# Grouped-query attention over a KV cache: loads of K, V and wo with wider DRAM pieces

## The chip, the core and the metric

The kernel runs on one core of a Trainium2 chip. The metric is the device time in microseconds (us) of one execution. The profile shows the engines of the core: PE (TensorE, with its weight loads shown apart as PEld), DVE (VectorE), ACT (ScalarE), POOL (GpSimd) and SP, the engine that here only issues DMAs. Sixteen DMA engines move the data between DRAM and SBUF.

## What is computed

It is one attention block for decoding with a cache, in bf16, with B = 32 batches of Sq = 4 new tokens, D = 1024, 32 query heads, 4 kv heads, 2048 cached positions and head size 128.

```python
B, Sq, D = 32, 4, 1024
Hq, Hkv, Sk, Dh = 32, 4, 2048, 128
q = (x @ wq).reshape(B, Sq, Hq, Dh)            # x: [B, Sq, D], wq: [D, Hq*Dh]
k = repeat(k_cache, Hq // Hkv, axis=heads)     # k_cache, v_cache: [B, Hkv, Sk, Dh]
v = repeat(v_cache, Hq // Hkv, axis=heads)
p = softmax(q @ k.T * Dh ** -0.5, axis=-1)
o = p @ v
out = o.reshape(B, Sq, Hq * Dh) @ wo           # wo: [Hq*Dh, D]
```

The two caches hold 67 MB each, wq and wo 8.4 MB each; everything is read from DRAM once.

## The kernel before

The engines have a program each, written out by hand and tied together by counting semaphores; a function `plan` numbers the events of each engine beforehand, and `wait_ev` waits for such a number. One batch at a time goes through five steps on TensorE:

- `do_kt_fills`: K arrives with positions on the partitions and has to be transposed. For each of the 4 kv heads two fills of 8 transposes each go into one bank of a ring of four PSUM banks (ps_a, ps_b, ps_c, ps_o; line 320), and DVE or ACT copies each bank to KT_sb (lines 452 and 454).
- The scores: 16 matmuls into ps_s (line 405), all 32 heads times 4 tokens as 128 rows.
- DVE takes the row maximum (line 489), and ACT the exponential with its sum (line 547) into pp_sb.
- `do_tr_fills`: 16 matmuls against a diagonal matrix transpose and scale the probabilities (line 336), through the same ring.
- `do_pv`: 64 matmuls of the probabilities with V (line 354), copied to oT_sb.

The order on TensorE in batch i is: scores of i, `do_pv` of i - 1, `do_kt_fills` of i + 2, `do_tr_fills` of i. Ahead of the loop stand the transposition of x, the fills of batches 0 and 1 and the projection of q (line 379); after it come 64 matmuls with wo (line 426) and the store of the output.

**Loads.** K_sb has two buffers of a whole batch (2 MB) and V_sb three. In SBUF partition p of a batch and head holds positions 16p to 16p + 15, which are 4 KB in a row of DRAM. K comes in one DMA for each kv head (512 KB), and each head has a semaphore of its own; V comes in one DMA for each batch (2 MB). wo comes in 32 DMAs of 256 KB, one for each query head, in rows of 2 KB, into the SBUF space of wq. ACT issues the K of batches 0 and 1; SP issues everything else, in this order: x, the four parts of wq, K2, V0, K3, V1, and then for each batch b from 2 on V(b), K(b + 2) and one wo block. Before V(b) SP waits until `do_pv` of b - 3 has freed the buffer (line 273), and before K(b) for the last fill of b - 2 (line 278). Before the first wo block it waits for the end of the projection of q (line 266).

The lines of the access patterns and of the wait for V are these:

```python
def k_src(b):                                                    # L229
    return k_cache[b].rearrange("g (p t) d -> p g (t d)", p=128)
...
eng.dma_start(V_sb[:, vs, :, :], v_src(b)).then_inc(s_v[vs], 16) # L274
...
eng.wait_ge(s_v[vs], 16 * (b // NVB + 1))                        # L347, do_pv
```

## Time and profile before

| | |
|---|---|
| time, median of 2 runs | 413.37 us (413.29 to 413.44) |
| the profiled execution | 413.86 us, of which the span of the instructions is 412.1 us |
| granted clock of TensorE | 0.917 of full speed, mean |
| busy: PE, PEld | 316.0 us (77%), 257.4 us (62%) |
| busy: DVE, ACT, POOL | 247.1 us (60%), 198.6 us (48%), 0.7 us |
| DMA | 152.33 MB in 44437 packets, mean 370 GB/s over the span |

Busy time is the time in which an engine executes instructions; its share of the span is an average over parts of the kernel with different limits. The span runs from the first to the last instruction; the time of an execution also has some 1.8 us around it. The profile cuts the span into 40 slices of 10.3 us and gives for each the busy tenths of every engine and the GB/s that the DMA engines moved. Its chain is the work that ended last, followed back from the last instruction to whatever released each step.

### The profile page before, as it was taken

The page shows a single profiled execution, that of the slowest core. Times are in us where ns is not written, and L with a number is a line of the kernel's source. Part 1 is how long each engine was busy: PE and PEld are TensorE (multiplying, and loading weights), DVE is VectorE, ACT ScalarE, POOL GpSimd, SP SyncE. Part 2 cuts the span into 40 slices and gives each one's busy share as a digit, 9 for nine tenths or more (in the row PEclk, how much of TensorE's full clock was granted, in tenths as well). Part 3 has the DMA queues.
Part 4 walks back from the last instruction along what each step waited for, and adds up shares of the span by engine and source line. Part 5 has one row for each costly group of instructions (what it writes and reads, how often), then busy time and mean ns, then how long its engine had stood idle before and what let it go on. Part 6 is the DMA issues. An engine that isn't in the chain of part 4 may idle for free.

```text
span 412.1 us, 12650 instructions
## 1 busy us (share of the span) xinstructions
PE 316.0 (77%) x5448; PEld 257.4 (62%) x5448; DVE 247.1 (60%) x390; ACT 198.6 (48%) x230; POOL 0.7 (0%) x6
## 2 busy tenths in 40 slices
PE   4489787887886986897787787777788787776596
PEld 3489576676665864775576665656576566665442
DVE  2114686775865786586677577667657667754500
ACT  1213655643645475455555355555535555534400
POOL 0000000000000000000000000000000000000000
PEclk9889998988989899699989899999979989978679
DMA  8999999999999999999999999999999999996000
GB/s 303 400 387 400 409 409 405 407 406 407 406 407 408 405 408 406 407 407 407 406 406 407 407 403 407 406 406 406 406 408 406 407 408 406 405 406 251 6 2 25
DMA packets 44437, 152.33 MB, mean 370 GB/s; under 512 B 3168, under 2 KB 3168, under 8 KB 44384
## 3 DMA queue, kind: packets, MB, share of 16 engines
q1 hardware_dynamic: 43232, 147.34, 90.5%
q10 hardware_dynamic: 1152, 4.19, 2.6%
q8 instruction: 44, 0.72, 0.7%
q14 instruction: 9, 0.07, 0.0%
HBM read 151.26 MB, written 0.26 MB: 368 GB/s over the span
## 4 chain that ended last, share of the span: by engine, by line
DMA 61%; PE 25%; SPq 5%; ACT 4%; issue 3%; DVE 2%; ACTq 0%; DVEq 0%
DMA K_sb<-in_k_cache_dram 55%; DMA w_sb<-in_wq_dram 6%; PE ps_c L320 4%; SPq L280 4%; PE ps_s L426 4%; PE ps_o L320 3%; PE ps_a L320 3%; ACT KT_sb L454 3%; PE ps_b L320 3%; PE ps_s L379 3%; DVE mx L489 2%; PE ps_s L405 1%; PE ps_o L354 1%; PE ps_a L336 1%; PE ps_o L336 1%
## 5 line engine op out<-in xcount | busy, mean ns | idle before, releaser
L547 ACT ACTIVATE pp_sb<-ps_s,negmx 128x2048 bf16<-128x2048 f32 x32 | 63.0, 1967 | 98.5 <-DVE negmx L492 98.5
L489 DVE TENSOR_REDUCE mx<-ps_s 128x1 f32<-128x2048 f32 x32 | 73.3, 2292 | 43.3 <-PE ps_s L405 43.3
L320 PE MATMUL ps_a<-ident,K_sb 128*128 128x128 bf16 x512 | 45.9, 240 | 31.9 <-DMA K_sb<-in_k_cache_dram 27.6
L354 PEld LDWEIGHTS ps_o<-pp_sb,V_sb 128*128 128x128 bf16 x2048 | 53.8, 96 | 17.9 <-issue 17.9
L454 ACT ACTIVATE KT_sb<-ps_a 128x1024 bf16<-128x1024 bf16 x32 | 32.7, 1023 | 59.1 <-PE ps_a L320 59.1
L354 PE MATMUL ps_o<-pp_sb,V_sb 128*128 128x32 bf16 x2048 | 57.2, 177 | 3.9 <-issue 3.0
L320 PEld LDWEIGHTS ps_a<-ident,K_sb 128*128 128x128 bf16 x512 | 34.8, 109 | 38.1 <-DMA K_sb<-in_k_cache_dram 32.5
L320 PE MATMUL ps_c<-ident,K_sb 128*128 128x128 bf16 x512 | 46.3, 242 | 12.6 <-DMA K_sb<-in_k_cache_dram 11.5
L452 DVE COPY KT_sb<-ps_b 128x1024 bf16<-128x1024 bf16 x64 | 43.9, 686 | 9.8 <-PE ps_b L320 9.0
L320 PEld LDWEIGHTS ps_c<-ident,K_sb 128*128 128x128 bf16 x512 | 35.7, 110 | 18.9 <-DMA K_sb<-in_k_cache_dram 17.2
L320 PE MATMUL ps_o<-ident,K_sb 128*128 128x128 bf16 x512 | 45.0, 238 | 2.2 <-DVE KT_sb L452 2.0
L320 PE MATMUL ps_b<-ident,K_sb 128*128 128x128 bf16 x512 | 45.3, 239 | 1.0 <-issue 1.0
L320 PEld LDWEIGHTS ps_o<-ident,K_sb 128*128 128x128 bf16 x512 | 36.4, 109 | 3.7 <-DVE KT_sb L452 3.0
L320 PEld LDWEIGHTS ps_b<-ident,K_sb 128*128 128x128 bf16 x512 | 36.8, 109 | 1.3 <-issue 1.2
L452 DVE COPY KT_sb<-ps_a 128x1024 bf16<-128x1024 bf16 x32 | 22.1, 691 | 24.8 <-PE ps_a L320 24.8
L405 PE MATMUL ps_s<-KT_sb,QT_sb 128*32 128x512 bf16 x512 | 34.3, 388 | 2.5 <-ACT QT_sb L530 0.8
L454 ACT ACTIVATE KT_sb<-ps_c 128x1024 bf16<-128x1024 bf16 x32 | 32.7, 1023 | 7.1 <-PE ps_c L320 7.0
L452 DVE CAST pp_sb<-ps_a 128x512 bf16<-128x512 f32 x32 | 22.1, 692 | 20.2 <-PE ps_a L336 20.2
L454 ACT ACTIVATE KT_sb<-ps_o 128x1024 bf16<-128x1024 bf16 x32 | 32.7, 1021 | 0.0
L452 DVE COPY KT_sb<-ps_c 128x1024 bf16<-128x1024 bf16 x32 | 22.1, 690 | 8.4 <-PE ps_c L320 8.3
L336 PE MATMUL ps_o<-diag,pp_sb 128*128 128x128 bf16 x128 | 13.2, 227 | 14.9 <-ACT KT_sb L454 14.9
L452 DVE CAST pp_sb<-ps_c 128x512 bf16<-128x512 f32 x32 | 22.1, 690 | 3.7 <-PE ps_c L336 1.4
(34 smaller groups left out, 245.2 us busy)
## 6 DMA issues: line engine op xcount, KB each, us to landing
V_sb<-in_v_cache_dram SPq DMA_DIRECT2D x32, 2048.0 KB, 19.2
K_sb<-in_k_cache_dram SPq DMA_DIRECT2D x120, 512.0 KB, 15.8
w_sb<-in_wq_dram SPq DMA_DIRECT2D x4, 2048.0 KB, 23.6
w_sb<-in_wo_dram SPq DMA_DIRECT2D x32, 256.0 KB, 14.7
K_sb<-in_k_cache_dram ACTq DMA_DIRECT2D x8, 512.0 KB, 10.6
pp_sb<-in_x_dram SPq DMA_DIRECT2D x1, 256.0 KB, 4.2
out_dram<-pp_sb SPq DMA_DIRECT2D x1, 256.0 KB, 2.0
```

The source lines that it names most:

```text
L280: eng.dma_start(K_sb[:, ks, g, :], k_src(b)[:, g, :]).then_inc(s_k[ks][g], 16)
L320: ins = eng.transpose(dst[:, q * 128:(q + 1) * 128], K_sb[:, ks, g, t * Dh:(t + 1) * Dh], ident[:, :],)
L336: ins = eng.matmul(dst[:, q * 128:(q + 1) * 128], lhsT=P_sb[:, t * 128:(t + 1) * 128], rhs=diag[:, b % 2, :], start=True, stop=True,)
L354: ins = eng.matmul(ps_o[:, 32 * g:32 * (g + 1)], lhsT=V_sb[:, vs, g, t * Dh:(t + 1) * Dh], rhs=PT_sb[:, t, 32 * g:32 * (g + 1)], start=(t ...
L379: ins = eng.matmul(ps_s[:, col:col + 128], lhsT=wq_sb[:, kt, h * Dh:(h + 1) * Dh], rhs=xT_sb[:, kt, :], start=(kt == 0), stop=(kt == KT - 1),)
L405: ins = eng.matmul(ps_s[32 * g:32 * (g + 1), c * 512:(c + 1) * 512], lhsT=QT_sb[:, i, REP * g:REP * (g + 1), :], rhs=KT_sb[:, kts, g, c * ...
L426: ins = eng.matmul(ps_s[:, c * 512:(c + 1) * 512], lhsT=oT_sb[:, h, :], rhs=wo_view[:, h, c * 512:(c + 1) * 512], start=(h == 0), stop=(h ...
L452: ins = eng.tensor_copy(dst, src)
L454: ins = eng.activation(dst, src, ACT.Copy)
L489: ins = eng.tensor_reduce(mx[:, i:i + 1], ps_s[:, :], AX.X, ALU.max)
L547: ins = eng.activation(P_sb, ps_s[:, :], ACT.Exp, bias=negmx[:, i:i + 1], scale=scale, accum_out=ssum[:, i:i + 1],)
```

## The change

A helper `_load` issues a DMA whose source and destination have different shapes and the same number of elements. The source patterns of K and V get 32 rows of 16 KB in place of 128 rows of 4 KB, and that of a wo block 16 rows of 16 KB in place of 128 rows of 2 KB; the destinations stay at 128 partitions with 4 KB (2 KB) each. Read in order, the elements of both sides match, so each byte goes to the same place as before. V is issued head by head, four DMAs of 512 KB for a batch, all of which raise the same semaphore; `do_pv` waits for four times the count.

```diff
+def _load(nc, eng, dst, src):
+    return eng.add_instruction(mybir.InstDMACopy(
+        name=nc.get_next_instruction_name(),
+        engine=eng.engine,
+        mode="Copy",
+        queue={mybir.EngineType.SP: "qSPDynamicHW", mybir.EngineType.Activation: "qActDynamicHW"}[eng.engine],
+        cce_op=ALU.bypass,
+        ins=[eng.lower_ap_dma(src)[0]],
+        outs=[eng.lower_ap_dma(dst)[0]],
+    ))
...
         def k_src(b):
-            return k_cache[b].rearrange("g (p t) d -> p g (t d)", p=128)
+            return k_cache[b].rearrange("g (p t) d -> p g (t d)", p=32)
         def v_src(b):
-            return v_cache[b].rearrange("g (p t) d -> p g (t d)", p=128)
+            return v_cache[b].rearrange("g (p t) d -> p g (t d)", p=32)
...
-                    eng.dma_start(wo_view[:, h, :], wo[h * 128:(h + 1) * 128, :]).then_inc(s_wo, 16)
+                    _load(nc, eng, wo_view[:, h, :], wo[h * 128:(h + 1) * 128, :].rearrange("(p r) n -> p (r n)", r=8)).then_inc(s_wo, 16)
...
-                eng.dma_start(V_sb[:, vs, :, :], v_src(b)).then_inc(s_v[vs], 16)
+                for g in range(G):
+                    _load(nc, eng, V_sb[:, vs, g, :], v_src(b)[:, g, :]).then_inc(s_v[vs], 16)
...
-                    eng.dma_start(K_sb[:, ks, g, :], k_src(b)[:, g, :]).then_inc(s_k[ks][g], 16)
+                    _load(nc, eng, K_sb[:, ks, g, :], k_src(b)[:, g, :]).then_inc(s_k[ks][g], 16)
...
-                eng.wait_ge(s_v[vs], 16 * (b // NVB + 1))
+                eng.wait_ge(s_v[vs], 16 * G * (b // NVB + 1))
...
-                    eng.dma_start(K_sb[:, b % NKB, g, :], k_src(b)[:, g, :]).then_inc(s_k[b % NKB][g], 16)
+                    _load(nc, eng, K_sb[:, b % NKB, g, :], k_src(b)[:, g, :]).then_inc(s_k[b % NKB][g], 16)
```

The last pair of lines is ACT's issue of K0 and K1.

## The prediction

> **What bounds the kernel now.** I read the page's DMA rows first, then the chain of waits, then the table of busy time by stretch, and last the waits of TensorE on K_sb and the DMA issues.

> ```profile
> DMA  8999999999999999999999999999999999996000
> GB/s 303 400 387 400 409 409 405 407 406 407 406 407 408 405 408 406 407 407 407 406 406 407 407 403 407 406 406 406 406 408 406 407 408 406 405 406 251 6 2 25
> ...
> q1 hardware_dynamic: 43232, 147.34, 90.5%
> ...
> q8 instruction: 44, 0.72, 0.7%
> ...
> DMA 61%; PE 25%; SPq 5%; ACT 4%; issue 3%; DVE 2%; ACTq 0%; DVEq 0%
> ```

> The DMA engines are at 9 tenths in every slice from 10 us to 371 us, and the rate is flat at 403 to 409 GB/s there. Nothing on the compute side has a digit row as flat. The chain agrees: 61% of it is DMA, nearly all of it K loads.

> ```profile
> 20.00:32.00 12.00, 10.65 (x153) 10.48 (x152) 2.81 (x5) 1.20 (x2) 0.00 (x0) 0.82 1.05 387
> 36.00:42.00 6.00, 5.22 (x96) 4.98 (x97) 0.95 (x2) 1.19 (x2) 0.00 (x0) 1.00 1.03 410
> 160.00:200.00 40.00, 31.02 (x587) 25.72 (x576) 26.82 (x42) 20.26 (x24) 0.00 (x0) 0.91 1.03 407
> ```

> The columns are the stretch, its length, busy us of PE, PEld, DVE, ACT and POOL, the granted clock, the DMA share and GB/s. Here lies the number that I use most. From 20 to 32 us the weights wq come (rows of 2 KB), from 36 to 42 us K and V (rows of 4 KB), both with the DMA share at 1: the rate is 387 against 410 GB/s. Between 160 and 200 us PE is busy 31.0 of 40 us.

> ```profile
> 350.25 16.48 DMA K_sb<-in_k_cache_dram
> 366.78 1.03 PE ps_c L320 x8
> ...
> PE ps_a L320 <- DMA K_sb<-in_k_cache_dram: 27.6, 36, 3.1
> PE ps_c L320 <- DMA K_sb<-in_k_cache_dram: 11.5, 33, 1.7
> ...
> V_sb<-in_v_cache_dram SPq DMA_DIRECT2D x32, 2048.0 KB, 19.2
> K_sb<-in_k_cache_dram SPq DMA_DIRECT2D x120, 512.0 KB, 15.8
> ```

> The first two rows are of the chain (start, length, what): the last K (batch 31) lands at 366.73 us, and from there compute alone takes the span to 412.1, a tail of 45.4 us. The middle two: PE waits 27.6 + 11.5 = 39.1 us for K, or 1.3 us in each of the 30 batches whose K comes after the start. The last two: a K load lands 15.8 us after its issue although its 512 KB need 1.3 us at 407 GB/s, so some 14 us of transfers always stand ahead of it in the queue.

> So the end is: start of the stream (about 2.5 us), plus the time of all bytes up to K31, plus the tail.

> **A price of one row.** Each of the 16 engines moves its share row by row. 2048 B at 387/16 GB/s take 84.7 ns; 4096 B at 410/16 take 159.8, and I use 160.0 to stay near the slightly lower 409 of the slices. The difference, 75.3 ns for 2048 B, is 27.2 GB/s for one engine (435 for 16), and 9.3 ns are left over as a fixed cost of each row. Check over the stream up to K31, per engine: K0 to K31 and V0 to V29 are 62 x 512 / 16 = 1984 rows of 4 KB, 317.4 us; 27 wo blocks are 216 rows of 2 KB, 18.3; wq and x 264 rows, 22.4; semaphore writes of 190 DMAs, 1.8; the instruction queue 0.7% of the span, 2.9. The sum is 362.8, and 2.5 us of start make 365.3 against 366.7 measured.

> [...]

> **The change part by part.**

> Read side: four rows of K or V (eight of wo) become one piece of 16 KB. The bytes, their places in SBUF and the order of the loads stay. If the 9.3 ns go with the piece that is read, 16 KB take 4 x 150.7 + 9.3 = 612.1 ns instead of 640.0. Per engine up to K31 there are 1984/4 + 27 = 523 pieces: 320.1 us instead of 317.4 + 18.3 = 335.7, or -15.6. Unknown cost, bounded: with no fixed cost left 602.8 ns a piece, -20.4; with all of it kept by the 4 KB (2 KB) writes, 0; and if writes get in each other's way, above nothing (third rival). I take 612.1: the reads are what gets fewer[...].

> V as four loads: 90 more DMAs up to V29, each with one semaphore write on every engine, at 9.3 ns: +0.8 us. On SP, one issue becomes four. The shortest V issue without a full queue is 0.38 us (at 362.95), the shortest K issue 0.33, so SP needs about 1 us more per batch, and the K of two batches later and wo are queued behind it. The 14 us of transfers in the queue hide this; uncovered it would cost up to 32 us over the kernel. TensorE's wait for V goes to 64 instead of 16 on the same semaphore, for the same bytes in the same order; V lands in 19.2 us and is used three periods of 10.9 us after its slot was freed, so 13 us stand between.

> What is late next: the stream gains 14.8 / 30 = 0.5 us a batch, and PE waits 1.3 us a batch for K, so 0.8 us of wait remains and DMA stays the bound. In the start, 16 KB pieces of K0 and K1 (ACT's queue) stand between the 2 KB rows of x and wq; x may land a microsecond later than its 4.2, but q's first matmuls wait for wq at 18.4 us, so nothing follows. The tail after K31 is compute and keeps its 45.4 us; wo's rest lands with the stream before the output matmul, 26.8 us after K31.

> Sum: -15.6 + 0.8 = -14.8 us. The profiled execution took 413.86 us (span 412.1, 1.8 around it); 413.86 - 14.8 = 399.1, and against the median 413.37 it is 398.6.

> **The rivals.** For: the forecast, 0.60. The stream is at its limit, the limit has a part per row, and the slack behind it (1.3 us a batch) is larger than the gain.

> First rival, 0.17: the fixed cost stays wholly or mostly with the writes, whose number does not change. [...] If nothing goes, +0.8: 414.2. For it: the writes stay rows of one partition. Against: nothing shows that a write costs more than a read.

> Second rival, 0.23, on the other side: [...] If a quarter of a piece's time is lost so, it takes 602.8 x 1.25 + 9.3 = 763 ns, 523 x 0.763 + 0.8 = 399.8, +64: 477.5 us. It makes the kernel 2% slower (8.3 us) from 656 ns a piece, which is 7% of lost time. For it: the flat rate so far hangs on one layout, and the only 16 KB packets in the profile, the 44 of the instruction queue, occupy 0.7% of 16 x 412.1 us, 1.05 us each instead of 0.61. Against: those share their engines with the stream, which alone would lengthen them.

> **How the numbers follow.** The measurement tells about 2%. Faster by over 2% is the forecast and its upper part: 0.60. Within 2%: the first rival, 0.17. Slower: the second rival, 0.23. The likeliest case's own range is 394 (no fixed cost left) to 404 (two thirds of the gain). To leave out no more than 2 in 10, the range runs on through the first rival to 430[...]: left out are 0.17 above it and 0.02 below 394.

> **What would show it.** Right: the page's packet count falls from 44437 to about 17800 (32768 + 4096 rows become 8192 + 512, and 1536 semaphore writes come on top), the GB/s row stands at 420 to 427, K31's first use of ps_c falls near 352 us, PE's waits for K fall from 39 to about 24 us, and the tail stays at 45. First rival: the same packet count with 407 to 415 GB/s. Second: GB/s below 400 with the DMA share still at 1. Wrong altogether would be a DMA share under 0.9 in the slices before K31: then the queue ran dry, on SP's issues or on compute.

## The result, and the profile after

The changed kernel takes 457.66 us (454.27 and 461.06) against 413.37: a ratio of 1.107, 95% interval 1.072 to 1.143. The forecast was 398.6, and the range ended at 430. The profiled execution is the one of 461.06 us, with a span of 459.3. Ratios here and below compare fast executions alone, and the only slow one, 459.06 us of the kernel with wo alone in wide pieces, is left out.

From the page after the change, the GB/s row, the packets and the chain:

```profile
GB/s 329 389 387 416 410 368 369 365 362 364 350 355 348 348 358 361 360 365 357 345 359 360 354 352 343 344 357 369 357 345 351 344 347 360 342 340 251 61 1 23
DMA packets 17814, 152.34 MB, mean 332 GB/s; under 512 B 4704, under 2 KB 4704, under 8 KB 9056
...
DMA 71%; PE 20%; SPq 2%; DVE 2%; issue 2%; ACT 1%; DVEq 0%; ACTq 0%
```

The change did what it says: 17814 packets, where the prediction expected about 17800. But the rate is 340 to 369 GB/s from the sixth slice on, where it was 403 to 409. The table of stretches shows where it begins (stretch, length, busy us of PE, PEld, DVE, ACT, POOL, clock, DMA share, GB/s). The first three rows are the kernel before, the other five the changed one:

```profile
36.00:64.00 28.00, 22.07 (x425) 18.30 (x423) 17.98 (x28) 13.90 (x17) 0.00 (x0) 1.00 1.03 408
64.00:70.00 6.00, 5.79 (x72) 5.61 (x72) 3.81 (x9) 2.99 (x4) 0.00 (x0) 0.72 1.03 406
76.00:82.00 6.00, 4.72 (x72) 3.80 (x76) 4.51 (x9) 5.13 (x7) 0.00 (x0) 1.00 1.03 404
...
36.00:64.00 28.00, 21.72 (x423) 18.18 (x420) 17.98 (x27) 13.80 (x17) 0.00 (x0) 1.00 1.01 407
64.00:70.00 6.00, 5.53 (x77) 5.10 (x73) 3.88 (x8) 2.76 (x4) 0.00 (x0) 0.72 1.01 317
70.00:76.00 6.00, 4.04 (x97) 2.83 (x94) 4.03 (x5) 2.99 (x5) 0.00 (x0) 1.00 1.01 411
76.00:82.00 6.00, 3.65 (x56) 3.15 (x57) 3.58 (x7) 2.75 (x3) 0.00 (x0) 1.00 1.03 320
82.00:88.00 6.00, 4.60 (x107) 3.39 (x104) 3.67 (x3) 3.02 (x4) 0.00 (x0) 1.00 0.98 395
```

Two things are to be seen. Up to 64 us, with K and V in 16 KB pieces already, the rate is that of before, neither better nor worse. Then stretches of 6 us at about 320 and 400 take turns, while the DMA share stays at 1: the engines are occupied and move less. The granted clock of TensorE isn't what does it: the kernel before has 406 GB/s at a clock of 0.72, the changed one 320 at 1.00. The turns have the rhythm of the batches. SP's row of the timeline (start, length, what) shows the issue of the first wo block:

```profile
51.64 0.59 SPq L16 DMA_DIRECT2D w_sb<-in_wo_dram  x1
```

The block lands 18.6 us after the start of this issue, at 70.3 us, which is the end of the first disturbed stretch. The end of the chain (start, length, what) and two of PE's waits (total us, times, longest) show what this does to the last K:

```profile
390.62 22.34 DMA K_sb<-in_k_cache_dram
413.01 1.04 PE ps_c L335 x8
...
PE ps_a L335 <- DMA K_sb<-in_k_cache_dram: 52.2, 36, 3.1
PE ps_c L335 <- DMA K_sb<-in_k_cache_dram: 21.4, 36, 2.0
```

The chain's last K now lands at 412.96 us instead of 366.73, 46.2 us later; the tail after it is 46.3 us (45.4 before). So nearly all of the loss lies in the stream. PE's waits for K, in the last two rows, went from 39.1 to 73.6 us; its busy time rose from 316.0 to 329.5 us, at a mean granted clock of 0.881 instead of 0.917.

### The profile page after: what moved, and what is told of

It is laid out like the page before. It is cut to its first block, busy times and chain, and to the rows that moved or that the text cites. A ratio compares the mean times of both kernels' runs of the same rounds, so it can differ in the third digit from the quotient of the medians.

```text
span 459.3 us, 12744 instructions
## 1 busy us (share of the span) xinstructions
PE 329.5 (72%) x5446; PEld 269.8 (59%) x5448; DVE 248.9 (54%) x390; ACT 199.5 (43%) x230; POOL 0.7 (0%) x6
## 2 busy tenths in 40 slices
DMA packets 17814, 152.34 MB, mean 332 GB/s; under 512 B 4704, under 2 KB 4704, under 8 KB 9056
## 3 DMA queue, kind: packets, MB, share of 16 engines
q1 hardware_dynamic: 17376, 147.34, 90.4%
## 4 chain that ended last, share of the span: by engine, by line
DMA 71%; PE 20%; SPq 2%; DVE 2%; issue 2%; ACT 1%; DVEq 0%; ACTq 0%
DMA K_sb<-in_k_cache_dram 66%; DMA w_sb<-in_wq_dram 5%; PE ps_c L335 3%; PE ps_s L441 3%; PE ps_o L335 3%; PE ps_s L394 2%; SPq L16 2%; PE ps_a L335 2%; PE ps_b L335 2%; DVE mx L504 2%; PE ps_s L420 1%; PE ps_a L351 1%; PE ps_b L351 1%; PE ps_o L369 1%; DVE KT_sb L467 0%
## 5 line engine op out<-in xcount | busy, mean ns | idle before, releaser
L335 PE MATMUL ps_a<-ident,K_sb 128*128 128x128 bf16 x512 | 49.8, 253 | 56.3 <-DMA K_sb<-in_k_cache_dram 52.2
L335 PEld LDWEIGHTS ps_a<-ident,K_sb 128*128 128x128 bf16 x512 | 37.6, 115 | 63.3 <-DMA K_sb<-in_k_cache_dram 57.9
L335 PE MATMUL ps_c<-ident,K_sb 128*128 128x128 bf16 x512 | 49.9, 254 | 21.9 <-DMA K_sb<-in_k_cache_dram 21.4
L335 PEld LDWEIGHTS ps_c<-ident,K_sb 128*128 128x128 bf16 x512 | 38.6, 116 | 28.8 <-DMA K_sb<-in_k_cache_dram 28.4
L467 DVE COPY KT_sb<-ps_b 128x1024 bf16<-128x1024 bf16 x64 | 44.0, 688 | 19.2 <-PE ps_b L335 18.8
L335 PE MATMUL ps_b<-ident,K_sb 128*128 128x128 bf16 x512 | 49.1, 252 | 0.0
L335 PE MATMUL ps_o<-ident,K_sb 128*128 128x128 bf16 x512 | 47.8, 248 | 1.4 <-DVE KT_sb L467 1.0
L335 PEld LDWEIGHTS ps_o<-ident,K_sb 128*128 128x128 bf16 x512 | 39.5, 114 | 2.5 <-DVE KT_sb L467 1.4
L335 PEld LDWEIGHTS ps_b<-ident,K_sb 128*128 128x128 bf16 x512 | 40.8, 117 | 0.1
## 6 DMA issues: line engine op xcount, KB each, us to landing
V_sb<-in_v_cache_dram SPq DMA_DIRECT2D x128, 512.0 KB, 19.5
K_sb<-in_k_cache_dram SPq DMA_DIRECT2D x120, 512.0 KB, 20.5
w_sb<-in_wq_dram SPq DMA_DIRECT2D x4, 2048.0 KB, 23.0
K_sb<-in_k_cache_dram ACTq DMA_DIRECT2D x8, 512.0 KB, 8.4
```

The costliest lines, as they stand in the source:

```text
L335: ins = eng.transpose(dst[:, q * 128:(q + 1) * 128], K_sb[:, ks, g, t * Dh:(t + 1) * Dh], ident[:, :],)
L467: ins = eng.tensor_copy(dst, src)
```

## The experiments

**Which part of the change.** Four kernels test three theories: that the wo blocks do it (A), that the wide K and V pieces do (B), or that the four V loads do (C).

First, wo alone goes back to rows of 2 KB:

```diff
-_load(nc, eng, wo_view[:, h, :], wo[h * 128:(h + 1) * 128, :].rearrange("(p r) n -> p (r n)", r=8)).then_inc(s_wo, 16)
+eng.dma_start(wo_view[:, h, :], wo[h * 128:(h + 1) * 128, :]).then_inc(s_wo, 16)
```

> K and V stay in 16 KB pieces with V in four loads; wo goes back to rows of 2 KB. Theory A (the wo blocks, 16 source rows against 128 partitions, disturb the stream; K and V in 16 KB pieces cost what four rows of 4 KB cost, 640 ns): 411 to 415 us, and the GB/s row at 403 to 411 in every slice from 42 us on. Theory B (the wide K and V pieces get in each other's way as the engines drift apart, wo has nothing to do with it): 445 to 460 us, GB/s near 355. Theory C (four V loads on SP delay the stream): 445 to 460 us, with a DMA share under 1.

Measured: 413.25 us against 412.74 for the kernel before, ratio 1.0004 (0.9987 to 1.0020). The whole loss is gone, and B and C with it, since this kernel keeps the wide K and V pieces and the four V loads. There is no sign of the gain that I had forecast: K and V in 16 KB pieces are worth nothing that can be measured. Over the long middle of both kernels the rate is the same (kernel before, then this one):

```profile
60.00:360.00 300.00, 236.03 (x4319) 194.41 (x4308) 205.28 (x324) 163.49 (x189) 0.00 (x0) 0.93 1.03 407
60.00:360.00 300.00, 234.80 (x4320) 193.15 (x4316) 204.52 (x324) 163.45 (x190) 0.00 (x0) 0.94 1.01 407
```

Second, the other way round: the kernel before, with wo alone in 16 KB pieces (the same edit, reversed).

> The kernel before with only the wo blocks read in 16 KB pieces; K, V and the number of V loads as before. Theory A: most of the loss is here, 435 to 460 us, although only 6% of the bytes changed. Theory B and C: 411 to 415 us.

Measured: 451.7 to 455.6 us against 412.74, ratio 1.097 (1.092 to 1.103). Over the same middle stretch:

```profile
60.00:360.00 300.00, 216.78 (x3852) 179.18 (x3844) 183.77 (x288) 146.73 (x169) 0.00 (x0) 0.91 1.03 362
```

The 6% of the bytes that are wo pull a stream of 4 KB rows from 407 to 362 GB/s. By the ratio the loss is 40.2 us, or 1.26 us for each of the 32 blocks, longer than a block needs when undisturbed (256 KB at 387 GB/s are 0.68 us).

In this kernel the wo pieces are the only 16 KB pieces of SP's queue, so its packed trace, which has the start, size and duration of each packet, shows them apart. The 16 pieces of the first block start between 65.4 and 67.9 us. The 4 KB rows of K and V that start between 66 and 67 us take 277 ns in the mean; from 58 to 64 us, and again from 70 to 76 us, they take 164. From 45 us on, summed and divided by 16 engines, the rows of K and V take 36.6 us more than in the kernel before, the wo pieces themselves only 5.2 us more. What is lost is lost mostly by the loads beside the block.

Third, all of the change, but wo in 32 pieces of 8 KB instead of 16 of 16 KB:

```diff
-wo[h * 128:(h + 1) * 128, :].rearrange("(p r) n -> p (r n)", r=8)
+wo[h * 128:(h + 1) * 128, :].rearrange("(p r) n -> p (r n)", r=4)
```

Theory A has two forms here: that the 16 source rows disturb the stream, or that any wide wo piece does.

> All of the change, but a wo block is read in 32 pieces of 8 KB, each filling 4 partitions as K and V do, instead of 16 pieces of 16 KB filling 8. Theory A[...]: 411 to 416 us, no disturbed stretches. Theory A in the form that any wide wo piece disturbs: 435 us or more. Theory B and C: 450 to 460 us.

Measured: 412.77 us, ratio 0.9998 (0.9982 to 1.0014). It isn't a wide wo piece as such. What is left is the piece that feeds eight writes, or the number of 16 pieces.

Fourth, the kernel before with only V split (`do_pv` then waits for four times the count):

```diff
-eng.dma_start(V_sb[:, vs, :, :], v_src(b)).then_inc(s_v[vs], 16)
+for g in range(G):
+    eng.dma_start(V_sb[:, vs, g, :], v_src(b)[:, g, :]).then_inc(s_v[vs], 16)
```

> The kernel before with only V split into four loads of 512 KB with rows of 4 KB. Theory A and B: 413 to 415 us (up to 0.8 us for the 96 more DMAs). Theory C: 430 us or more.

Measured: 412.99 us, ratio 1.0000 (0.9985 to 1.0016). Theory C fails by itself too, and the 0.8 us of semaphore writes are at most 0.7.

**Width or place.** The next question is whether a 16 KB piece with eight writes blocks an engine, or whether the shape of the load is the matter, its 16 source rows against 128 partitions. If it is the shape, two halves of 64 partitions may disturb the stream as well, with nothing wide in them; if it is the width, they don't. In the kernel before, with rows of 2 KB, each wo block is cut into two loads of 64 partitions (and the wait for wo counts two loads for each block):

```diff
-eng.dma_start(wo_view[:, h, :], wo[h * 128:(h + 1) * 128, :]).then_inc(s_wo, 16)
+for hp in range(2):
+    eng.dma_start(wo_view[64 * hp:64 * (hp + 1), h, :],
+                  wo[h * 128 + 64 * hp:h * 128 + 64 * (hp + 1), :]).then_inc(s_wo, 16)
```

> The kernel before, with rows of 2 KB throughout, but each wo block is loaded by two DMAs of 64 partitions each (0 to 63, 64 to 127). Nothing is read in wide pieces. [...] the stream is disturbed as with the wide wo blocks, 430 to 455 us. Width theory (it is the 16 KB piece with eight writes behind one read that blocks an engine): 412 to 416 us.

Measured: 458.85 us, ratio 1.111 (1.106 to 1.115). Nothing in this kernel is wide, and it loses as much as the change. That it issues 32 more DMAs can't be the reason: 96 more cost nothing in the run before. Its disturbed and quiet stretches stand as after the change:

```profile
64.00:70.00 6.00, 4.45 (x76) 3.85 (x72) 3.89 (x8) 3.03 (x4) 0.00 (x0) 1.00 1.03 328
70.00:76.00 6.00, 4.00 (x97) 2.79 (x94) 4.03 (x5) 2.90 (x5) 0.00 (x0) 1.00 1.02 407
```

The dose: the change, with every second wo block in rows of 2 KB again (`if h % 2 == 0` around the wide load).

> The change with every second wo block in rows of 2 KB again: 16 wide wo blocks instead of 32. If each wide block costs a fixed piece of time (some 1.2 us[...]): 413 + 16 x 1.3 = 430 to 436 us. If the disturbance is a lasting drift of the engines that the first blocks set off: near 455 us.

Measured: 432.3 us, ratio 1.046 (1.042 to 1.050): 19.7 us for 16 blocks, 1.23 us each. A slice of this run is as long as a batch, and its GB/s row shows single wide blocks from the seventh slice on:

```profile
GB/s 326 391 386 414 408 404 368 402 361 410 360 405 354 406 387 389 383 378 397 360 408 358 405 360 402 371 388 382 373 384 378 392 367 404 356 387 292 50 2 24
```

From the seventh to the fourteenth slice, and again from the twentieth to the twenty-fifth, about 360 and 405 take turns; in between, the slices and the batches are out of step. A block costs its time and leaves nothing behind.

Then K and V themselves in 16 pieces, of 32 KB (`p=16` in k_src and v_src), wo in rows of 2 KB. If 16 source rows disturb a load beside others of their kind too, all of the stream is slow, for which the expectation's first range is an estimate:

> K and V are read in 16 pieces of 32 KB, each filling 8 partitions, as wo was in the change; wo in rows of 2 KB. [...] 520 to 720 us (GB/s 220 to 330). Width theory: twice as wide a piece, but with no other kind beside it; 413 us if only the mixture hurts, above 460 if the width does.

Measured, in one run: 594.6 us. From 60 to 400 us it runs at 272 GB/s with the DMA share at 1.01. That is two thirds of 407:

```profile
60.00:400.00 340.00, 206.47 (x3233) 168.65 (x3232) 155.56 (x243) 123.73 (x143) 0.00 (x0) 0.79 1.01 272
```

**Where the fixed cost of a row lies.** Two bursts: all wo blocks issued together (`issue_wo(Hq if b == 6 else 0)`), so that some 20 us of the stream are pure wo; once in the kernel before, in rows of 2 KB, and once in the changed kernel, in 8 KB pieces that each feed four writes of 2 KB.

> The kernel before, with all 32 wo blocks (rows of 2 KB) issued one behind the other after K of batch 8, so that one stretch of some 20 us is pure wo: 387 GB/s in that stretch, as wq has. The total stays near 413 us or rises by what PE idles there and can't make up.

> The same burst, with K, V and wo in wide pieces, wo in 8 KB pieces that each fill 4 partitions with 2 KB. If the fixed 9.3 ns belong to the read piece: 8192 B in 310.6 ns, 422 GB/s in the pure wo stretch. If they belong to each write: 4 x 84.7 = 339 ns, 387 GB/s, as in the burst with rows of 2 KB.

Measured, in one run each: 416.43 and 415.94 us. The burst, first in rows of 2 KB, then in 8 KB pieces:

```profile
110.00:126.00 16.00, 5.05 (x112) 3.85 (x112) 4.67 (x7) 5.55 (x7) 0.00 (x0) 0.80 1.06 387
110.00:126.00 16.00, 5.05 (x112) 3.85 (x112) 4.46 (x6) 5.40 (x7) 0.00 (x0) 0.77 1.02 387
```

387 and 387: a quarter of the reads, the same rate. In this pair of runs the cost goes with the writes. The packets of K and V say the same: in the run with wo plain and K and V wide, a 16 KB piece takes 640 ns in the median (after 45 us), as long as the prediction's four rows of 4 KB and not the forecast 612.1.

Last, longer rows on both sides. wq in full rows of 8 KB, which makes the projection of q wait for all of wq:

```diff
-for c in range(NWQC):
-    eng.dma_start(wq_sb[:, :, c * WQC:(c + 1) * WQC], wq_v[:, :, c * WQC:(c + 1) * WQC]).then_inc(s_wq[c], 16)
+for kt in range(KT):
+    eng.dma_start(wq_sb[:, kt, :], wq_v[:, kt, :]).then_inc(s_wq[0], 16)
```

> The kernel before, but wq is loaded by 8 DMAs of full rows of 8 KB, contiguous on both sides, in place of 4 DMAs with rows of 2 KB; the projection of q waits for all of wq. If a fixed cost of 9.3 ns goes with each write however long it is, an 8 KB row takes 310.6 ns and the stretch of pure wq runs at 422 GB/s; if the engine pays for each 4 KB, 320 ns and 410 GB/s. The bytes of wq then come 1.8 or 1.2 us sooner: 411 to 413 us if the later start of the projection is hidden by the queue of K and V, and 415 to 420 us if not.

Measured: 415.6 us, ratio 1.0076 (1.0054 to 1.0098). Its stretch of pure wq, and the stretch that spoils it:

```profile
20.00:30.00 10.00, 0.00 (x0) 0.00 (x0) 0.00 (x0) 0.00 (x0) 0.00 (x0) 1.00 1.02 419
42.00:52.00 10.00, 10.00 (x182) 9.93 (x180) 4.46 (x7) 4.05 (x5) 0.00 (x0) 1.00 0.46 174
```

8 KB rows run at 419 GB/s, 313 ns for a row, near the 310.6 of one fixed cost and clear of the 320 of two 4 KB rows. So in these runs one write has one fixed cost up to 8 KB at least. But the projection now starts only at 33.9 us, and the fills of batch 1 that stand among its matmuls end at 47.3. SP holds K3 back behind them until 47.5, the queue runs dry (DMA share 0.46), and the kernel ends later.

The milder form has wq in two halves of columns, rows of 4 KB (`WQC = 2048`):

> The kernel before, with wq in two DMAs of half its columns (rows of 4 KB on both sides) instead of four of a quarter (2 KB). 2048 rows fewer at 9.3 ns on 16 engines are 1.2 us of stream. The projection of q starts later by some 4 us, but not so late that the queue runs dry: 412 us, a ratio of 0.997. If the queue runs dry all the same, 414 us or more. If the cost goes with reads and writes of 4 KB alike and not with rows, 413.

Measured: 412.24 us against 412.93, ratio 0.9977 (0.9962 to 0.9992). It is about 1 us faster than the kernel before, and its stretch from 20 to 32 us runs at 408 GB/s instead of 387:

```profile
20.00:32.00 12.00, 8.03 (x110) 8.03 (x111) 1.27 (x2) 0.60 (x1) 0.00 (x0) 0.67 1.02 408
```

## Why the prediction was wrong

Two steps failed: the saving of -15.6 us for fewer reads, which measured 0, and the shape of the wo loads (16 source rows for 128 partitions), whose cost the sum put at nothing and which measured 44.3 us.

**The bound** was read rightly. The stream sets the end: 46 of the 47 us of the profiled run are in the landing of K31, and the tail moved by 0.9.

**The price of a row** was right as a sum and put on the wrong side. The prediction had fixed 9.3 ns a row from two sizes and then chose: "the reads are what gets fewer". The two sizes could not decide this, because reads and writes of a row were equally long in both. The bursts decide it: 387 against 387 GB/s, where the read side would have given 422. The term of -15.6 us measured 0: K and V, 13.8 of it, with a ratio of 1.0004 (wo plain, between 0.5 us below and 0.8 us above the kernel before), and K, V and wo together with 0.9998 (wo in 8 KB pieces). That was the first rival's case of nothing gained, given 0.17 for all or most of the cost staying with the writes.

**The second rival** was the one that came, in its kind and not in its place. It said that the writes would get in each other's way, and priced that as a quarter of the time of all 523 pieces, K and V above all: +64 us. How they would do so was the author's assumption, and no run shows it. Its sign, under 400 GB/s with the DMA share still at 1, is what the profile shows (317 GB/s at a share of 1.01 from 64 to 70 us). But K and V with 32 source rows are as undisturbed as with 128 (407 GB/s in both from 60 to 360 us); the whole loss comes with the 32 wo blocks. That the measured 44.3 us fall between the forecast and this rival is therefore no confirmation of its sum. The step that failed is the one that gave pieces of K and V and pieces of wo one price: 32 source rows against 128 partitions measured 0, 16 source rows 1.2 to 1.4 us a block.

The price of a block was put at some 1.2 us before the run with every second block, an estimate of the author's, whose parts no run shows. Measured were 1.23, 1.26 and 1.38 us a block (every other block wide, wo alone wide, the change) and 1.45 for the halves of 64 partitions. That the sum fits doesn't show where the time goes: with wo alone wide, the wo pieces take 845 ns in the mean, about 160 more than eight rows of 2 KB, and seven eighths of the loss are in the rows of K and V.

Shown is that wo loads of 16 source rows, or of 64 partitions, slow down the stream: six runs agree on it (wo plain, wo alone wide, wo in 8 KB pieces, halves of 64 partitions, every other block, K and V in 16 rows), and the halves, in rows of 2 KB, exclude the width of the piece. Not shown is how the two shapes do it. The profile doesn't name the engine of a packet, so which partitions each engine writes and which DRAM rows it reads was not seen. No run changes the writes alone, so a cause on the DRAM side stays as open as one on the side of SBUF.

**Minor steps.** V's four loads and SP's issues were hidden, as costed (0.8 us forecast, -0.6 to +0.7 measured). That the early x and wq would not matter held: the projection of q ends with a matmul that starts at 40.8 us, where it was 40.7.

## What to carry to other kernels

A fixed cost that is fitted from rows of two lengths, equally long on both sides, says nothing on which side of the transfer pays it; change one side alone in a short burst before building on it. When source and destination of a load have different numbers of rows, try each of the shapes alone beside the stream: here 32 rows against 128 partitions were free (ratio 0.9998), and 16 rows, or 64 partitions, cost 1.2 to 1.5 us for each 256 KB, about twice the time of the bytes themselves (0.68 us at 387 GB/s). A DMA share of 1 with a falling GB/s was the sign of it here (1.01 at 317 GB/s).
